# Turning activation rows on TensorE instead of by DMA, and folding late row pairs before the transform back over p

## The chip, the core and the metric

The kernel runs on one core of one Trainium2 chip. The metric is the device time of one execution in microseconds (us). Runs of one kernel agree here within some tenths of a per cent.

## The reference, cut to what matters

Two kinds of layer, A and B, alternate on a state `x` of 2048 rows and 512 columns in bfloat16: A, B, A, B. A is a two-dimensional Fourier filter, B is a small MLP that mixes neighbouring rows.

```python
def _A_ref(x, w_r, w_i):
    X = rfft2(x) * (w_r + 1j * w_i)
    return irfft2(X, s=(S, D))

def _B_ref(x, w1, w2, w3, w4):
    h = gelu(layernorm(x) @ w1)
    # g0..g3: the four column quarters of h, shifted by -1, +1, -2, +2 rows
    x1 = x + concatenate([g0, g1, g2, g3]) @ w2
    return x1 + gelu(layernorm(x1) @ w3) @ w4

x = x + _A_ref(layernorm(x)); x = x + _B_ref(layernorm(x))
x = x + _A_ref(layernorm(x)); x = x + _B_ref(layernorm(x))
```

## The kernel before, in words

The 2048 rows are written as 16 p + q with 128 values of p (the partitions) and 16 values of q. A "row" below is one q: a tile of 128 partitions by 512 columns. The state `K.x` holds the 16 rows in SBUF for the whole run.

`first_front` makes the first half of the first Fourier transform; then `layer` runs twice, each time finishing an A and doing a B, and the first run also makes the front of the next A. One run of `layer` goes through these stages:

- The filter: `over_d`, `over_q`, the product with `W` in `weigh`, `back_q`, and copies out of PSUM between them.
- The way back. `back_d` (L662) makes four rows of columns for a pair of rows in two PSUM banks: an even part in the first 256 columns and an odd part in the last 256. `take_D` copies the pair to SBUF as `Y`. `back_p` (L690) transforms a row back over p with four matmuls of 256 columns: the left half of the row is even plus odd part, the right half even minus odd, and both sums are formed in PSUM. `add_x` (L698) adds to the state, `stats2` (L303) squares on ScalarE, `rstd2` forms the inverse deviation on GpSimd, and `norm2` (L400 on VectorE and GpSimd, L402 on ScalarE) makes the normalized row `xn`.
- The turn. A matmul contracts over partitions, so the normalized rows must be turned so that the columns of the row lie on the partitions. `tr` (for `w1`) and `tr3` (for `w3`) call `turn` for a pair of rows, and `turn` issues one DMA transpose on SyncE's queue (L718) from `xn` into `xT`. There are 8 of each in a layer.
- The MLP. `w1` (L733), `gelu1` (L740), `w2` (L749), `add_x1` (L757), `square3`, `rstd3`, `norm3`, then `w3` (L784) with `gelu3` (L791) and `w4` (L804) with `add_x2` (L810) and, in the last layer, `store` (L814).
- In the first run of `layer`, scaled tables (`scale_T`, L410/L412) and `front` (L429, L439) of the next A are interleaved with the last matmuls of `w4`.

Nothing is scheduled by the compiler. Three strings, `ORDER_0`, `ORDER_A` and `ORDER_B`, list the operations by one letter and a number, and each engine executes its own operations in that order. A trailing A, V, P or D names the engine, and ".b" names the first PSUM bank. The letters used below: D and C `back_d`, Y `take_D`, P `back_p`, a `add_x`, s `stats2`, n `norm2`, T `tr`, v `w1`, h `gelu1`, u `w2`, U `tr3`, w `w3`, W `w4`. X is `fill`: so many matmuls on a zero tile (L274) whose result nobody reads. Every engine waits for its inputs in order, so one instruction that waits holds up all that stand behind it on its engine.

The options `half_D` (K) and `fold_D` (H) stand in the kernel before but are not used: `FOLD` is empty for both layers.

Of the kernel before, what the change touches and what calls it, by code (L numbers as in the profile page):

```python
# [28 lines left out]
def dft_tables():  # L29
# [12 lines left out]
    p = np.arange(P)  # L42
    pair = lambda j, s: (j if s == 0 else 64 - j) if j else 32 * s
    T = np.zeros((P, NH, 2, 2))
    for j in range(NH):
        for s in range(2):
            i = pair(j, s)
            T[:, j, s, 0] = np.cos(2 * np.pi * i * p / 128)
            T[:, j, s, 1] = np.sin(2 * np.pi * i * p / 128) if i else np.cos(np.pi * p)
    T = T.reshape(P, P)  # L50
    d = np.arange(D // 2)
    f = np.arange(1, 257)
# [9 lines left out]
    w = np.full(256, 2.0)  # L62
    w[255] = 1.0
    G = np.stack([cos * w, sin * w]) / (S * D)
    G = G.transpose(2, 0, 1).reshape(2, P, 2, D // 2).transpose(1, 0, 2, 3)
    A = np.zeros((NH, NQ, 2, 2, 2, 32))
    B = np.zeros((NH, NQ, 2, 2, 2, 32))
    q = np.arange(NQ)
    for j in range(NH):
        for sg in range(2):  # L70
            for m in range(32):
                k = 64 * m + (j if sg == 0 else 64 - j if j else 32)
# [24 lines left out]
           "Tinv": np.stack([T.T, -T.T], axis=1)}  # L97
# [43 lines left out]
def banks(K, n):  # L141

    k = K.bank
    if k is None:
        k = K.next_bank if K.next_bank + n <= 8 else 0
        K.next_bank = (k + n) % 8
    return K.ps[:, k:k + n, :]


def copy(K, dst, src, eng):  # L150
    if eng == "V":
        K.nc.vector.tensor_copy(dst, src)  # L152
    else:
        K.nc.scalar.activation(dst, src, ACT.Copy, bias=0.0, scale=1.0)  # L154


def load_all(K, A_x, A_w_r, A_w_i, B_w1, B_w2, B_w3, B_w4):
# [16 lines left out]
    for pl, v in enumerate(planes):  # L174
        nc.scalar.dma_start(K.W[2::4, pl, 0], v[:, 32])
    for lo in range(0, NH, 8):
        for pl, v in enumerate(planes):
            load_W(K, v, pl, lo, lo + 8)
    K.TL = K.const.tile([P, 2, NB, P], BF16, name="TL")
# [28 lines left out]
    def load_mlp():  # L208
        gate2 = K.const.tile([1, 16], BF16, name="gate2")
        nc.sync.dma_start(gate2[:], K.W[1:2, 1, NH - 1, 1:17])  # L210
        for k in ("G", "Tinv"):
            table(k, nc.sync)
        for k, w, n, c in (("w1", B_w1, 4, D), ("w2", B_w2, 4, D), ("w3", B_w3, 4, FH), ("w4", B_w4, 14, D)):
            t = K.const.tile([P, n, c], BF16, name=k)
            setattr(K, k, t)
            if k != "w4":
                load_halves(t, w, n)

    def load_w4():
        load_halves(K.w4, B_w4, 14)  # L220

    def load_halves(t, w, n):
        v = w.rearrange("(t p) n -> p t n", p=P)
        for part in (slice(0, n // 2), slice(n // 2, n)):
            nc.sync.dma_start(t[:, part], v[:, part])

    K.load_w4 = load_w4
# [10 lines left out]
def load_W(K, v, pl, lo, hi):  # L238


    j1 = max(lo, 1)
    fwd, rev = [K.W[2 * sg::4, pl] for sg in range(2)]
    K.nc.sync.dma_start(fwd[:, lo:hi], v[:, lo:hi])
    K.nc.sync.dma_start(rev[:, j1:hi], v[:, 65 - hi:65 - j1][:, ::-1])
# [243 lines left out]
def first_front(K):  # L488
# [66 lines left out]
    dummy = K.const.tile([P, 1, P], BF16, name="dummy")  # L555
    K.nc.sync.dma_start_transpose(dummy[:], K.zeros[:])
# [11 lines left out]
def layer(K, last):  # L568
# [144 lines left out]
    def turn(to, k, rows):  # L713

        g, h = divmod(k, 2)
        if g not in to:
            to[g] = K.grp.tile([P, 4, 4, P], BF16, name="xT", bufs=4)
        nc.sync.dma_start_transpose(to[g][:, 2 * h:2 * h + 2].rearrange("p q t c -> p (q t) c"),  # L718
                                    rows.rearrange("p q d -> p (q d)"))

    def tr(k):
        turn(xT, k, xn[:, 2 * k:2 * k + 2, :])
        turned.append(k)
        if len(turned) == 8 and not last:
            K.load_w4()
# [48 lines left out]
    def tr3(k):  # L774
        q = ROWS[2 * k]
        turn(xT3, k, xn[:, q:q + 2, :])
# [84 lines left out]
    def act_table(k):  # L861
# [4 lines left out]
    next_V, turned = {}, []  # L866
    table = {"z": act_table, "e": lambda g: ln[g].std_twice(), "i": lambda g: ln[g].invert_twice(), "M": lambda g: ln[g].shift(), "J": invert4, "d": over_d, "t": take_d, "q": over_q, "x": take_q, "p": weigh, "b": lambda b: back_q(b, first_half(b)), "V": lambda b: back_q(b, 1),
             "D": lambda m: back_d(m, 0), "C": lambda m: back_d(m, 1), "Y": take_D, "P": back_p, "a": add_x, "s": stats2, "r": rstd2, "c": lambda g: ln[g].ratio(), "n": norm2,
             "T": tr, "v": w1, "h": gelu1, "u": w2, "f": add_x1, "k": square3, "E": resid,
# [34 lines left out]
FLEX = "mlGLnotxYIKEpQ"  # L904
FOLD = [(), ()]
ORDER_0 = """
s1 f0 s0 s3 s2 i3 i2 i0 s4 s5 S1 J1 s7 S0 J0 s6 i7 f2 Q2A Q3A i4 Q0A s9 i6 s8 O1.2 s11 f3 S2 J2 Q6P Q1A Q5A O0.4 i8
G1A Q4V O2.0 s10 i11 i10 S3 Q7P O3.2 G0A s13 J3 Q10V Q11A s12 s14 i12 O5.6 i14 G3A i13 G2A Q8P Q9P s15 S4 J4 O4.4 G5A
i15 Q12V Q13V S5 O6.0 L5A J5 Q14P O7.6 G4A G6A G3V Q15V L6V G7A O8.0 L7A G8A I3V L8A
"""  # L910
ORDER_A = """
d0.3 t0A d2.4 d1.2 d4.0 q0.6 t1V N0 t2A q1.2 d6.4 t4A q2.0 x1V x0V p1V t6A q4.2 d12.6 d10.4 x2A p2P p0V t12A t10A d8.0
p4D b0.6 d14.7 q10.4 m0V q6.2 t8A x10A t14A b1.0 b5.1 m5A m1A q12.4 q14.6 p6D b4.1 b2.0 p10V x14A p14P d15.2 m4A m2A
t15A q8.6 x8A b3.1 b7.0 m7A b11.2 q15.6 m11A x15A b10.3 b14.0 m3A b6.2 m6A p12D V12.4 b12.5 p8V p15V b13.7 b9.1 m10A
m12A b8.6 b15.2 m13V V15.3 m14V m9A m8V V13.5 V14.0 m15A D1.6 l12V D0.1 l15A l13A l14V C1 C0 Y0V Y1A D3.3 C3 P3.0 a3
P2.6 Y3A a2 s3 P0.5 a0 s2 P1.2 a1 s0 D2.0 C2 Y2V s1 r0 D5.6 C5 P7.2 a7 Y5A e0 s7 P6.4 D7.0 P4.5 a6 i0 M0 P5.2 D4.6 C4
P10.3 s6 C7 n2P a4 s4 a5 n3V n0V s5 Y4A D6.4 r1 P11.2 C6 P8.6 P9.7 e1 n1V a10 T1 Y7A P15.0 i1 M1 n5A s10 n4P n6P P14.1
Y6V P13.3 a8 s8 T0 a9 n7P s9 a11 P12.4 a15 s11 v1.6 r2 n10P T2 h1 T3 a13 a12 n11V c0 s15 T5 n8V v0.2 h0 s13 v3.4 n9V
v2.2 h3 u0.0 s12 h2 u1.4 a14 c1 s14 T4 u3.1 r3 f0 k0 n14V v5.2 n13A n15V T7 f1 E1V h5 f3 v4.6 u2.0 f2 E2V h4 c2 u6.6
f6 u5.5 f5 E5V k3 E6V n12P u7.0 E0V u4.1 f4 T6 v7.5 k2 k1 R0 E3V o2V o1V h7 o3A c3 v6.1 h6 o0P f7 u8.0 f8 E8P u13.5  # L920
u12.2 u11.6 u14.3 U1 f12 k4 k5 k7 f14 E14V k12 k6 u9.2 f11 u10.4 k8 E7V f13 k13 f10 R1 o7P o5P u15.3 E10V U0 w4.0 E4P
f9 E9P k11 f15 w2.4 g2 k10 o4V U2 w1.2 k14 g4 E15P k9 E13P w3.6 g3 g1 w5.0 w0.4 g0 w6.6 g5 g6 E11V W1.2 o6P U3 E12V A1
W3.6 A3 B3 B1 w8.0 W2.4 A2 W0.2 k15 R2 o10P o11A R3 o14V o9A g8 o12A w13.0 U5 w7.6 B2 g13 o8P U4 w15.4 w10.0 A0 B0 g10
w16.2 j1 g7 g16 w18.0 g18 w9.2 o15P w11.0 g9 w12.2 g12 j3 w17.6 j2 j0 S0 Q3V Q1V Q2P Q0V g11 W4.2 U7 O1.0 o13P g17 U6
A4 W7.3 B4 j4 G1A G1V A7 B7 j7 O0.0 w19.6 G0A W6.2 A6 g19 W5.3 A5 g15 B5 w23.4 g23 j5 B6 j6 S1 Q4P G0V w27.2 g27 I0V
w14.6 g14 Q5V O2.0 w20.2 w24.6 g20 W10.2 A10 B10 Q7V j10 W8.3 G2A A8 B8 W9.4 A9 B9 Q6V j9 W11.2 A11 w26.4 I1P B11 j11
g24 j8 O3.2 w22.6 S2 Q10P g26 G2V I2P Q11A Q8P g22 w21.0 g21 G3A w25.6 G3V g25 W12.0 A12 B12 j12 Q9P S12 J12 I3P O4.5
G4A Q12A G4V W15.1 A15 I4P B15 j15 W13.2 A13 S15 J15 B13 j13 W14.3 Q15P W24.2 S13 J13 Q13P O5.0 A14 A24 B14 B24 j14
G5A O15.4 G15V O6.2 S14 J14 L15A Q14A O14.4 G6A L6A G14A G5V I5V L14A
"""  # L930
# [47 lines left out]
```

## Time and profile before

| | us |
|---|---|
| median of three runs | 343.75 (343.66 to 343.83) |
| the profiled execution | 343.63 |
| its span, first to last instruction | 341.8 |
| TensorE (PE) busy | 334.3 (98%) |
| ScalarE (ACT) busy | 192.0 |
| VectorE (DVE) busy | 163.5 |
| GpSimd (POOL) busy | 117.5 |

The profiled execution takes 1.83 us more than its span. The busy time of PE is a sum over pipelined matmuls whose ends are modelled, so what a matmul costs is better read from the distance between the starts of consecutive ones. The granted TensorE clock is 1.000 in the whole execution.

The parts of the span, by the starts of PE's stages:

| stretch, us | work of PE |
|---|---|
| 0 to 18.96 | first front |
| 18.96 to 36.85 | filter of the first layer |
| 36.85 to 51.16 | way back up to the first `w1` |
| 51.16 to 79.08 | `w1`, `w2` |
| 79.08 to 181.59 | `w3`, `w4`, front of the next layer |
| 181.59 to 199.36 | filter of the second layer |
| 199.36 to 214.57 | way back up to the first `w1` |
| 214.57 to 242.37 | `w1`, `w2` |
| 242.37 to 341.8 | `w3`, `w4`, stores |

### The profile page before, as it was taken

The numbers are of one execution on the slowest core, as the hardware profiler recorded it, in microseconds if no ns is written. First come the engines' busy times: TensorE is split into PE (matmuls) and PEld (weight loads), VectorE is DVE, ScalarE is ACT, GpSimd is POOL, SyncE is SP. The second block draws the span as 40 slices with busy tenths as digits, with TensorE's granted clock in tenths as the row PEclk, the third lists the DMA queues.
The fourth block names the chain that finished last, engine by engine and source line by source line (L and its number), as shares of the span: only waits on it lengthen the run. The fifth ranks groups of instructions, "written<-read, shape, count | busy, mean of one in ns | idle before, by whom it ended". The sixth has DMA issues, their size and how long they took to land.

```text
span 341.8 us, 5734 instructions
## 1 busy us (share of the span) xinstructions
PE 334.3 (98%) x2184; PEld 186.8 (55%) x2184; DVE 163.5 (48%) x373; ACT 192.0 (56%) x356; POOL 117.5 (34%) x218
## 2 busy tenths in 40 slices
PE   6999999999999999999999999999999999999996
PEld 4878984444444444444467898444444444444443
DVE  4979895659034023535378979456901110200112
ACT  6989899665821542421628979986695132142310
POOL 3795067669633000402432505877722000000000
PEclk9999999999999999999999999999999999999999
DMA  7985936390231100000000003543130500000011
GB/s 261 313 284 197 339 78 117 71 270 19 46 61 31 32 0 0 2 0 0 2 0 2 2 3 64 104 83 61 33 61 0 125 31 0 15 17 32 15 63 46
DMA packets 45340, 24.60 MB, mean 72 GB/s; under 512 B 35153, under 2 KB 42321, under 8 KB 45313
## 3 DMA queue, kind: packets, MB, share of 16 engines
q1 hardware_dynamic: 43824, 19.74, 23.0%
q0 software_dynamic: 1248, 4.40, 3.9%
q8 instruction: 17, 0.28, 0.3%
q10 hardware_dynamic: 240, 0.10, 0.1%
q14 instruction: 11, 0.08, 0.1%
HBM read 11.61 MB, written 2.10 MB: 40 GB/s over the span
## 4 chain that ended last, share of the span: by engine, by line
PE 85%; ACT 8%; DVE 3%; DMA 2%; issue 1%; SPq 0%; ACTq 0%
PE ps L804 28%; PE ps L784 28%; PE ps L749 8%; PE ps L733 6%; PE ps L642 4%; ACT xn L303 3%; PE ps L612 2%; PE ps L594 2%; DVE x_state L698 2%; PE ps L662 2%; DMA x_state<-in_A_x_dram 1%; ACT hT L740 1%; DMA xT<-xn 1%; PE ps L439 1%; PE ps L429 1%
## 5 line engine op out<-in xcount | busy, mean ns | idle before, releaser
L791 ACT ACTIVATE gT<-ps 128x1024 bf16<-128x1024 f32 x56 | 55.7, 1023 | 97.6 <-PE ps L784 95.5
L804 PE MATMUL ps<-w,gT 128*128 128x512 bf16 (+2 forms) x476 | 99.4, 366 | 0.0
L784 PE MATMUL ps<-xT,w 128*128 128x512 bf16 x448 | 99.3, 379 | 0.0
L810 DVE TENSOR_TENSOR x_state<-ps,x_state 128x512 bf16<-128x512 f32 (+2 forms) x34 | 22.1, 659 | 123.4 <-PE ps L804 123.1
L804 PEld LDWEIGHTS <-gT 128*128 128x128 bf16 x476 | 45.4, 98 | 51.4
L784 PEld LDWEIGHTS <-w 128*128 128x128 bf16 x448 | 43.7, 98 | 52.1
L757 DVE SCALAR_TENSOR_TENSOR xn<-xn,ln_c,ps 128x512 bf16<-128x512 bf16 x32 | 23.3, 742 | 16.0 <-PE ps L749 6.3
L733 PE MATMUL ps<-xT,w 128*128 128x512 bf16 x128 | 28.6, 379 | 0.4 <-DMA xT<-xn 0.4
L749 PE MATMUL ps<-w,hT 128*128 128x512 bf16 x128 | 28.8, 379 | 0.1
L326 POOL TENSOR_SCALAR ln_ve<-ln_mv 128x4 f32<-128x4 f32 x11 | 3.0, 271 | 57.7 <-DVE ln_mv L319 57.0
L303 ACT ACTIVATE junk<-xn 128x512 bf16<-128x512 bf16 x32 | 19.8, 623 | 5.0 <-DVE xn L757 5.0
L291 DVE BATCH_NORM_STATS2 ln_st<-x_state 128x6 f32<-128x512 bf16 (+2 forms) x30 | 19.5, 665 | 3.5 <-DMA x_state<-in_A_x_dram 3.0
L698 DVE SCALAR_TENSOR_TENSOR x_state<-ps,x_state 128x512 bf16<-128x512 f32 x32 | 20.6, 684 | 0.9 <-PE ps L690 0.9
L733 PEld LDWEIGHTS <-w 128*128 128x128 bf16 x128 | 12.4, 98 | 15.6 <-DMA xT<-xn 1.0
L749 PEld LDWEIGHTS <-hT 128*128 128x128 bf16 x128 | 12.5, 98 | 15.4 <-ACT hT L740 1.0
L303 ACT ACTIVATE xn<-x_state 128x512 bf16<-128x512 bf16 x32 | 19.9, 626 | 0.8 <-DVE x_state L698 0.8
L740 ACT ACTIVATE hT<-ps 128x512 bf16<-128x512 f32 x32 | 17.6, 600 | 4.6 <-PE ps L733 4.5
L690 PE MATMUL ps<-Y,Tinv 128*128 128x256 bf16 x128 | 15.8, 272 | 0.4 <-DVE Y L152 0.4
L631 POOL TENSOR_TENSOR PB<-X,W 128x2048 bf16<-128x2048 bf16 (+1 forms) x4 | 12.1, 3033 | 11.2 <-DVE X L152 7.3
L154 ACT ACTIVATE TV<-ps 128x1024 bf16<-128x1024 f32 (+1 forms) x17 | 14.6, 895 | 2.4 <-PE ps L594 2.3
L642 PE MATMUL ps<-TR,PB 128*128 128x128 bf16 x256 | 15.9, 219 | 0.0
L662 PE MATMUL ps<-G,hT 128*128 128x256 bf16 x128 | 15.6, 273 | 0.0
(96 smaller groups left out, 414.0 us busy)
## 6 DMA issues: line engine op xcount, KB each, us to landing
w<-in_B_w_dram SPq DMA_DIRECT2D x4, 896.0 KB, 7.0
W<-W POOLq DMA_DIRECT2D x4, 514.0 KB, 5.1
x_state<-in_A_x_dram SPq DMA_DIRECT2D x8, 256.0 KB, 4.9
out_dram<-x_state SPq DMA_DIRECT2D x15, 128.0 KB, 1.8
w<-in_B_w_dram SPq DMA_DIRECT2D x4, 256.0 KB, 4.4
W<-in_A_w_r_dram SPq DMA_DIRECT2D x7, 128.5 KB, 5.4
W<-in_A_w_i_dram SPq DMA_DIRECT2D x7, 128.5 KB, 5.6
TL<-tab_TL POOLq DMA_DIRECT2D x3, 256.0 KB, 5.5
```

The source lines that it names most:

```text
L303: K.nc.scalar.activation(out, src, ACT.Square, bias=0.0, scale=D ** -0.5, accum_out=self.s[:, i, 1:2])
L642: nc.tensor.matmul(o[:, k0 * P:(k0 + 1) * P], lhsT=pab[u][:, k, 2 * (b - u) + h, f * P:(f + 1) * P], rhs=K.TR[:, k:k + 2, 2 * b + h], star ...
L662: nc.tensor.matmul(o[:, i, e * 256:(e + 1) * 256], lhsT=M[:, F, e, 2 * m + i, :], rhs=K.G[:, F, e, :], start=(F == 0 and e == 0), stop=(F ...
L698: nc.vector.scalar_tensor_tensor(K.x[:, q, :], ps.pop(("P", q)), 1.0, K.x[:, q, :], op0=ALU.mult, op1=ALU.add, accum_out=ln[g].s[:, i, 0:1])
L733: nc.tensor.matmul(o[:, i], lhsT=K.w1[:, t, j * P:(j + 1) * P], rhs=xT[g][:, :, t, :], start=(t == 0), stop=(t == 3))
L740: nc.scalar.activation(hv[:, 2 * h + i, 4 * g:4 * g + 4, PAD:PAD + P], o[:, i].rearrange("p (q c) -> p q c", q=4), ACT.Gelu_apprx_tanh, bi ...
L749: nc.tensor.matmul(o, lhsT=K.hT[:, j, st:st + P], rhs=K.w2[:, j, :], start=(j == 0), stop=(j == 3))
L757: nc.vector.scalar_tensor_tensor(xn[:, q, :], xn[:, q, :], ln[q // 4].c[:, q % 4:q % 4 + 1], ps.pop(("u", n)), op0=ALU.mult, op1=ALU.add, ...
L784: nc.tensor.matmul(o[:, i], lhsT=K.w3[:, c, t * P:(t + 1) * P], rhs=xT3[g][:, :, c, :], start=(c == 0), stop=(c == 3))
L791: nc.scalar.activation(gT[g][:, 2 * j:2 * j + 2, :], ps.pop(("w", k)), ACT.Gelu_apprx_tanh, bias=0.0, scale=1.0)
L804: nc.tensor.matmul(o, lhsT=gT[g][:, t, i * P:(i + 1) * P], rhs=K.w4[:, t, d], start=(t == 0), stop=(t == 13))
L810: nc.vector.tensor_tensor(x, ps.pop(("W", n)), x, op=ALU.add)
```

## The change

`turn` no longer issues a DMA. It runs eight matmuls for a pair of rows: each has a block of 128 by 128 of `xn` as the stationary operand and a new 128 by 128 identity table `unit` as the moving one, and the turned pair lies in two PSUM banks. A new operation (Z for `tr`, F for `tr3`) copies the two banks to `xT` on ScalarE or VectorE.

`FOLD` becomes (4, 5, 6, 7) in both layers. For these row pairs, `half_D` copies the odd part to SBUF in float32 and `fold_D` forms sum and difference on VectorE, in place of `take_D`; `back_p` then needs two matmuls of 256 columns instead of four.

On the queues: the two small loads of `W` (16 KB each) move from ScalarE's queue to SyncE's, behind the first four loads of `W`; the load of `w4` moves from behind the eighth transpose to directly behind the load of `w3`; the dummy transpose goes; the load of `unit` (32 KB) is added before the weights. SyncE's queue then holds only loads and the final stores.

All three order strings are written anew. Apart from Z, F, K and H the operations are the same; some move to another engine and many to another place.

```diff
-           "Tinv": np.stack([T.T, -T.T], axis=1)}
+           "Tinv": np.stack([T.T, -T.T], axis=1), "unit": np.eye(P)}
...
-    for pl, v in enumerate(planes):
-        nc.scalar.dma_start(K.W[2::4, pl, 0], v[:, 32])
     for lo in range(0, NH, 8):
         for pl, v in enumerate(planes):
             load_W(K, v, pl, lo, lo + 8)
+        if lo == 0:
+            for pl, v in enumerate(planes):
+                nc.sync.dma_start(K.W[2::4, pl, 0], v[:, 32])
...
-        for k in ("G", "Tinv"):
+        for k in ("G", "Tinv", "unit"):
             table(k, nc.sync)
...
-            if k != "w4":
-                load_halves(t, w, n)
-
-    def load_w4():
-        load_halves(K.w4, B_w4, 14)
+            load_halves(t, w, n)
...
-    dummy = K.const.tile([P, 1, P], BF16, name="dummy")
-    K.nc.sync.dma_start_transpose(dummy[:], K.zeros[:])
...
-    def turn(to, k, rows):
-
-        g, h = divmod(k, 2)
+    def turn(key, rows):
+
+        ps[key] = o = banks(K, 2)
+        for i in range(2):
+            for t in range(4):
+                nc.tensor.matmul(o[:, i, t * P:(t + 1) * P], lhsT=rows[:, i, t * P:(t + 1) * P], rhs=K.unit[:],
+                                 start=True, stop=True)
+
+    def take_turned(to, key, eng):
+        g, h = divmod(key[1], 2)
         if g not in to:
             to[g] = K.grp.tile([P, 4, 4, P], BF16, name="xT", bufs=4)
-        nc.sync.dma_start_transpose(to[g][:, 2 * h:2 * h + 2].rearrange("p q t c -> p (q t) c"),
-                                    rows.rearrange("p q d -> p (q d)"))
+        copy(K, to[g][:, 2 * h:2 * h + 2].rearrange("p q t c -> p q (t c)"), ps.pop(key), eng)
 
     def tr(k):
-        turn(xT, k, xn[:, 2 * k:2 * k + 2, :])
-        turned.append(k)
-        if len(turned) == 8 and not last:
-            K.load_w4()
+        turn(("T", k), xn[:, 2 * k:2 * k + 2, :])
...
-        turn(xT3, k, xn[:, q:q + 2, :])
+        turn(("U", k), xn[:, q:q + 2, :])
...
-FOLD = [(), ()]
+FOLD = [(4, 5, 6, 7), (4, 5, 6, 7)]
```

The new order of the first layer, from the first `back_d` to the first `w2`:

```
D1.4 l12V C1 D0.0 C0 D3.2 Y1A P3.6 a3 Y0A C3 D2.4 C2 s3 Y2A Y3V P1.6 P0.7 a1 P2.3 a0 s1 P6.2 a2 P4.6 a6 s0 s2 D5.4 C5
a4 K5A P7.3 a7 r0 D4.0 e0 i0 M0 n2P s6 s7 H5 P5.2 n3P C4 K4A X7.7 P10.3 T1.4 D7.6 a5 C7 H4 P9.2 s4 s5 Z1A n1V n0P T0.0
r1 K7A a10 e1 D6.4 C6 Z0A a9 P11.3 i1 M1 n5P K6A H7 n4P P8.2 H6 n6P v1.0 T2.6 n7P c0 P15.4 h1 a11 s9 a8 s8 P12.5 P13.3
a13 T3.0 Z3V v0.2 a15 Z2A s11 s10 P14.0 r2 a12 s12 a14 v3.6 h3 v2.0 h0 u0.4
```

and of the second, from the first `back_d` to the first `w1`:

```
D0.4 l15V l13A D2.0 l14A C0 C2 Y2A D1.2 C1 Y0V D3.6 C3 P4.1 P5.0 Y1V P3.2 Y3A P7.3 a4 s4 P6.4 a5 s5 D5.0 a7 s7 P2.5
a6 s6 P0.3 a3 a0 C5 r1 D4.6 s3 a2 P1.2 K5A a1 e1 i1 M1 s2 D7.4 s1 C7 C4 K4A n6P H5 X5.3 P10.2 s0 r0 n7V T3.0 H4 a10
n4A e0 i0 X6.3 P8.3 a8 n5P T2.6 P11.2 Z3A a11 M0 n0P Z2A K7A D6.0 C6 P9.3 n1V T0.6 n3P n2P a9 H7 v2.2
```

The fills are X6 at the head of the second layer before, and X3 (head of the first layer), X7, X5 and X6 after.

## The prediction

> **What bounds the kernel now.** I read the page first: the shares of the engines, the slices, then the chain that ended last.
>
> ```profile
> span 341.8 us, 5734 instructions
> PE 334.3 (98%) x2184; PEld 186.8 (55%) x2184; DVE 163.5 (48%) x373; ACT 192.0 (56%) x356; POOL 117.5 (34%) x218
> PE   6999999999999999999999999999999999999996
> PEclk9999999999999999999999999999999999999999
> PE 85%; ACT 8%; DVE 3%; DMA 2%; issue 1%; SPq 0%; ACTq 0%
> ```
>
> PE is busy in every slice but the first and the last, at full clock, and carries 85% of the chain. Busy alone could be matmuls that wait inside their pipeline, so I then took the distances between matmul starts, from the chain of waits in order of time:
>
> ```profile
> 142.44 0.45 PE ps L439 x8
> ...
> 160.60 5.18 PE ps L784 x24
> ...
> 181.59 0.66 PE ps L274 x6
> ...
> 202.15 0.90 PE ps L690 x8
> ```
>
> So 128 moving columns cost 56 ns (0.45/8), 256 cost 110 ns (0.90/8, 0.66/6), 512 cost 216 ns (5.18/24): cost goes with the columns, and a weight load of its own for each matmul (L439 has one too) does not show. PE is at its streaming rate. What is left of waiting inside the run is seen in PE's timeline:
>
> ```profile
> 48.21 2.80 PE L690 MATMUL ps<-Y,Tinv 128*128 128x256 bf16 x24
> 51.16 7.08 PE L733 MATMUL ps<-xT,w 128*128 128x512 bf16 x32 [0.15 <-DMA xT<-xn]
> ...
> 204.61 2.35 PE L662 MATMUL ps<-G,hT 128*128 128x256 bf16 x20
> 207.40 1.64 PE L690 MATMUL ps<-Y,Tinv 128*128 128x256 bf16 x12 [0.44 <-DVE Y L152]
> ...
> 211.50 2.78 PE L690 MATMUL ps<-Y,Tinv 128*128 128x256 bf16 x24
> 214.57 7.08 PE L733 MATMUL ps<-xT,w 128*128 128x512 bf16 x32 [0.29 <-DMA xT<-xn]
> ```
>
> From start to start, less the matmuls between at 109 to 110 ns, PE lost 0.3 us at 51.16, 0.6 at 207.40 and 0.4 at 214.57. Only the first and third are waits for a transpose. The waits table agrees on how little the transposes cost, and shows that ScalarE and VectorE wait for PE and not the other way round:
>
> ```profile
> DVE x_state L810 <- PE ps L804: 123.1, 27, 16.8
> ACT gT L791 <- PE ps L784: 95.5, 35, 12.8
> PEld L733 <- DMA xT<-xn: 1.0, 2, 0.6
> PE ps L733 <- DMA xT<-xn: 0.4, 2, 0.3
> ```
>
> The page's PE idle is 341.8 - 334.3 = 7.5 us; 1.0 of it lies before the first matmul, 1.9 + 0.5 + 0.3 in the front, 2.7 after the last matmul. About 1.1 us is left for the whole middle (a few tenths more when counted by starts). So nearly every matmul that is added must be paid, and nearly none can be hidden.
>
> **The change part by part.**
>
> *The turns on TensorE.* 8 T and 8 U in each of two layers are 32 turns of 8 matmuls, 256 in all, 128 moving columns each. By the L439 row (same operand sizes, own weights each time): 32 x 0.45 = 14.4 us. The 16 U stand among L784 and L804, where PE is busy without a gap from 79 to 181 and from 242 to 339 us: 7.2 us on the path in full. The 16 T stand among `back_p`, `w1` and `w2`, where PE is also busy in full but for the waits above: another 7.2. The nearest rule is in the Trainium skill, "TensorE: Matmul & The Clock Gate", Part 4 (PE-mode transpose): in its transpose mode about 275 ns for 128x128 in a kernel, and not counted as activity by the clock gate. By that, 256 x 0.275 = 70 us, with a cold clock on top. But the diff issues plain matmuls against an identity, and the row for such a shape says 56 ns at a clock of 1.00; the 219 ns that the same row gives as the mean of one L439 matmul is its latency, which overlaps. I take 14.4; its lower end is the same, since 128 columns cannot stream faster than the row, and its upper end 14.9 (L642, also 128 columns: 3.68 us for 64 at 33.19, 57.5 ns).
>
> *What the turns take away.* 32 DMA transposes, 3.1 us each to landing, and the dummy. They are off PE's path but for the 0.3 and 0.4 us above. The skill's "VectorE: DVE Perf Modes" (The three transpose paths) gives 1309 ns by DMA against 390 ns on TensorE for a 128x128 block and advises TensorE. By that, 256 x 0.92 = 235 us would be gained if all of it were waited for; the trace shows 0.4 us of PE waiting in 2 of 32. What is late next: turn, latency and copy are about 0.45 + 0.2 + 1.0 = 1.7 us against 3.1 to 3.5, so a `w1` can start about 1.5 us earlier only where its inputs were last; PE's own work then fills that place. The 0.7 us are set against the new waits below.
>
> *Copies out of PSUM.* 32 copies of 128x1024 float32 to bfloat16: 17 on ScalarE (like Y at L154, 1.01 us) and 15 on VectorE (L152, 1.22): 17 and 18 us. The 16 F lie where both engines mostly wait for PE (L791 and L810 above): nothing, covered by w3 and w4; if that cover were gone, 1 to 1.2 us each. The 16 Z lie in the stage from 36.85 to 79.08, where ScalarE is busy 33.7 of 42.2 us and VectorE 29.6; with 4.6 to 5 us more each they stay below PE, but around the first `w1` ScalarE has no slack (12.8 of 14.3 us).
>
> *The fold.* 16 rows lose two matmuls of 256 columns: 32 x 0.11 = 3.5 us less on PE, on the path. In place of 4 casts Y (1.0 to 1.2) per layer come 4 K (128x512 float32, like `right`, 0.59) and 8 halves of H (like L461, 0.68): some 3.5 us more per layer, on VectorE mostly. Cover: PE's deferred `back_p` (P8 to P15 now stand around and behind the first T and v).
>
> *Fills.* X7, X5 and X6 stand inside the way back: 18 x 0.11 = 2.0 us. PE executes them, so they are paid whether a wait would stand there or not. X3 at the head and the X6 that goes from the head of layer two lie in waits for the last copy of V (0.3 us idle at 18.96): nothing, either way; without them the wait remains.
>
> *New waits.* Walking the new order of layer one with the durations above from the first D: last `a` of rows 0 to 3 at 6.4 us, its square at 7.05, deviation and normalized rows 2 and 3 (both on GpSimd, 0.77 each) at 10.0; PE has 9.7 us of work before T1 (12 D/C x 0.44, 8 P x 0.44, 7 fills, one folded P): 0.3 us of wait. ScalarE then has K7, e1 and Z0 before v1 and ends at 14.1, PE is there at 13.6: 0.5. Through the table load (1.28) and h1, s, Z2, h3 to h0, which u0 needs: ScalarE 23.2, PE 22.85: 0.4. So 1.2 us against 0.6 before (0.3 at 51.16 and 0.3 among the L749 ahead of 60.95). In layer two T3 must wait for n7V, which stands behind H5: 11.4 against 10.35 of PE, 1.0 us; before it was 0.6 + 0.2 + 0.4. Both layers together: + 0.6 - 0.2 = + 0.4. These waits aren't in the trace: lower end -1.4 (all old ones go, none comes), upper end +4 (each of the four places in each layer later by half a square or copy, 0.5).
>
> *Queues and front.* ScalarE issues two DMAs less (L175, 1.2 us of its queue) but its first work waits for x, landing at 3.9 us: nothing; an earlier landing gives up to 0.2. SyncE's queue gets them, 1.2 us more of issue before the last W (issued to 17.8, doubled copies landed by 31.2): W for `weigh` and G, needed at 36.85 and landed at 34.7, keep 1 us of margin; if that goes, up to 1 us. `unit` (32 KB) and w4 go ahead of nothing that is needed sooner. The front has the same work in another order: 0, ±0.5.
>
> **Sum**, against the profiled 343.63 (span 341.8 + 1.83): + 14.4 (turns) - 3.5 (fold) + 2.0 (fills) + 0.4 (waits, new less old) = 356.9. The profiled execution lies 0.12 below the median of the runs shown: nothing to correct.
>
> **The rivals.**
> 1. *The work is as counted, the waits go* (0.22). The fills sit where waits would be and everything old is given back: 343.63 + 14.4 - 3.5 + 2.0 - 1.4 = 355.1; with half of the fills replaced by a better flow, 353.5 at the least. For it: fewer PE operations ahead of the first v. Against: ScalarE and VectorE get more work there.
> 2. *ScalarE and VectorE become the bound of the way back* (0.19). K, H and Z come when ScalarE was busy 12.8 of 14.3 us. If half of the additional 4.8 us per layer is not covered, + 2 x 2.4: about 361; with PSUM banks held longer, 364.
> 3. *Not slower* (0.02). TensorE would have to take the turns into time that it lost to the transposes: 14.4 + 2.0 - 3.5 = 12.9 us, 0.40 us for each turn. It decides from 12.9 us of hidden waiting; the trace has 0.3 + 0.4 by the starts and 7.5 in all. Were matmul ends hiding so much, L784 would not step at 216 ns. Time: 343.6 or less. That the turns are cheaper in some unseen way is in this chance.
>
> The likeliest (0.57) is 355.8 to 358.8. Range: 353.5 to 361.0, which holds rival 1 and the lower part of rival 2. A difference of 0.2% (0.7 us) is about what a measurement of this kernel tells from none. Faster 0.01, same 0.01, slower 0.98.
>
> **What would show it.** PE busy still 97 to 98%; a new group of 256 matmuls with `unit`, 8 in 0.45 us; L690 with 96 instead of 128; no DMA_TRANSPOSE; the stretches with w3 and w4 longer by 3.6 us per layer each; the way back plus w1/w2 longer by 3.6 - 1.75 + fills + waits, some 3.5 per layer; PE waits of 0.3 to 1 us ahead of T1, v1, u0 and T3, released by GpSimd or ScalarE. Wrong would be: turns at more than 60 ns each, idle of PE over 3 us in a way back, U waiting for a norm or a bank in the w3 stage, or a front that ends more than 1 us from 18.96.

## The result and the profile after

The changed kernel takes 358.31 us (median of four runs, 357.93 to 358.83); the kernel before took 343.71 us on the same chip (343.62 to 343.83). The ratio is 1.0425, with a 95% interval of 1.0407 to 1.0443. The change makes the kernel slower by 14.6 us. The prediction said 356.9 us and slower, in a range of 353.5 to 361.0.

The profiled execution of the changed kernel took 358.05 us, with a span of 356.3; before these were 343.63 and 341.8. The page of the changed kernel:

```profile
span 356.3 us, 6168 instructions
PE 348.0 (98%) x2423; PEld 199.6 (56%) x2423; DVE 186.0 (52%) x390; ACT 207.4 (58%) x376; POOL 115.3 (32%) x227
PE   6999999999999999999999999999999999999996
PEclk9999999999999999999999999999999999999999
PE 84%; ACT 8%; DVE 5%; issue 2%; DMA 1%; POOL 0%; DVEq 0%; ACTq 0%; POOLq 0%
```

The picture is that of before: PE is busy in every slice but the first and the last, at full clock, and carries 84% of the chain. Only the span is 14.5 us longer, and the number of matmuls has grown by 239: 256 for the turns, less 32 for the fold, and 21 fills in place of 6. Now the chain of waits of the changed kernel, in order of time, where two turns for `w3` stand between the `w3` themselves:

```profile
99.81 0.45 PE ps L711 x8
...
106.30 1.73 PE ps L780 x8
108.03 0.45 PE ps L711 x8
108.47 1.73 PE ps L780 x8
```

L711 is a turn, L780 `w3`. The second number is what the step took: eight matmuls of a turn take 0.45 us, whatever stands around them, and the `w3` step at the same 216 ns as before. Nothing overlaps: the chain goes from one to the other. The groups of the changed kernel by shape (busy time, mean ns of one):

```profile
L711 PE MATMUL ps<-unit,xn 128*128 128x128 bf16 x256 | 19.7, 219 | 0.3 <-POOL xn L395 0.2
L683 PE MATMUL ps<-Y,Tinv 128*128 128x256 bf16 x64 | 8.1, 273 | 0.0
L678 PE MATMUL ps<-Y,Tinv 128*128 128x256 bf16 x32 | 5.7, 272 | 0.0
```

The whole way back over p has 96 matmuls instead of 128 (the folded rows are L678, two each). The mean of 219 ns of a turn's matmul is its latency; its price is the 56 ns from one start to the next.

The parts of the span, by the starts of PE's stages. "Streaming" is the number of matmuls times their step (56 ns for 128 columns, 109 for 256, 163 for 384, 216 for 512; the half-height matmuls of `over_q` run two at a time, so a pair counts 109); "rest" is the length less that, so waits and all else. "Fills" are the X, which are in neither.

| stage | before, us | rest | after, us | rest |
|---|---|---|---|---|
| first front | 18.96 | | 19.21 | |
| filter, layer one | 17.89 | 1.97 | 17.84 | 1.92 |
| way back to the first `w1` | 14.31 | 0.34 | 13.83 | 0.82, and 0.76 of fills |
| `w1`, `w2` | 27.92 | 0.29 | 32.77 | 0.70 |
| `w3`, `w4`, next front | 103.00 | 0.30, and 0.66 of fills | 105.35 | 0.62 |
| filter, layer two | 17.28 | 1.36 | 18.14 | 2.22 |
| way back to the first `w1` | 15.21 | 1.24 | 14.91 | 1.02, and 1.20 of fills |
| `w1`, `w2` | 27.64 | 0.01 | 30.86 | 0.10 |
| `w3`, `w4` | 96.89 | 0.16 | 100.43 | 0.16 |
| after the last matmul | 2.70 | | 2.96 | |

The stages behind the filters, where streaming and rest are both counted, grew by 12.1 us of streaming and fills (256 turns' matmuls 14.3, fold -3.5, fills 1.96 - 0.66) and by 1.1 of rest; the two filters, the front and the end grew by 1.3 together. That is the 14.5. A stage does not hold the same work before and after: in each layer only six of the eight turns for `w3` stand in the `w3`, `w4` stage, the other two stand ahead of the first `w3`; and in layer two four matmuls of `w2` (0.86 us) have come to stand behind the first `w3`.

Where PE still waits is seen in its timeline of the changed kernel, around the way back of layer one and of layer two. The columns are start and length in us, then the group; a bracket is the idle time before it and what ended it:

```profile
45.87 0.93 PE L269 MATMUL ps<-zeros 128*128 128x256 bf16 x7
46.63 0.48 PE L678 MATMUL ps<-Y,Tinv 128*128 128x256 bf16 x2
46.95 0.92 PE L711 MATMUL ps<-unit,xn 128*128 128x128 bf16 x8
...
50.16 0.60 PE L678 MATMUL ps<-Y,Tinv 128*128 128x256 bf16 x4
50.88 1.89 PE L729 MATMUL ps<-xT,w 128*128 128x512 bf16 x8
...
72.38 1.90 PE L729 MATMUL ps<-xT,w 128*128 128x512 bf16 x8 [0.27 <-DVE xT L152]
...
216.87 0.71 PE L269 MATMUL ps<-zeros 128*128 128x256 bf16 x5
...
217.77 0.61 PE L711 MATMUL ps<-unit,xn 128*128 128x128 bf16 x8
...
219.28 0.38 PE L711 MATMUL ps<-unit,xn 128*128 128x128 bf16 x4
219.82 0.40 PE L711 MATMUL ps<-unit,xn 128*128 128x128 bf16 x4 [0.16 <-POOL xn L395]
...
222.04 1.89 PE L729 MATMUL ps<-xT,w 128*128 128x512 bf16 x8
```

By the starts, 0.30 us are lost inside the turn at 46.95, 0.28 ahead of the `w1` at 50.88 (50.16 and four steps of 109 ns make 50.60), 0.43 before 72.38, 0.32 between the two halves of the turn at 219.28 and 0.19 inside the one at 221.39. The turn at 217.77, the first of layer two, does not wait. The waits table of the changed kernel (us in total, times, longest) agrees that these are small, and shows what hides the new copies:

```profile
DVE x_state L806 <- PE ps L800: 107.7, 24, 14.4
ACT gT L787 <- PE ps L780: 81.4, 33, 7.3
PEld L729 <- DVE xT L152: 0.8, 1, 0.8
PEld L711 <- POOL xn L395: 0.6, 2, 0.3
```

VectorE waited 123.1 us for `w4` before and waits 107.7 now, ScalarE 95.5 us for `w3` before and 81.4 now: the copies F have gone into time in which both waited for PE anyway.

### The profile page after: what moved, and what is told of

The parts are those of the page before. It is cut to its first block, busy times and chain, and to the rows that moved or that the text cites. A ratio compares the mean times of both kernels' runs of the same rounds, so it can differ in the third digit from the quotient of the medians.

```text
span 356.3 us, 6168 instructions
## 1 busy us (share of the span) xinstructions
PE 348.0 (98%) x2423; PEld 199.6 (56%) x2423; DVE 186.0 (52%) x390; ACT 207.4 (58%) x376; POOL 115.3 (32%) x227
## 2 busy tenths in 40 slices
DMA packets 11534, 16.25 MB, mean 46 GB/s; under 512 B 1344, under 2 KB 8512, under 8 KB 11504
## 4 chain that ended last, share of the span: by engine, by line
PE 84%; ACT 8%; DVE 5%; issue 2%; DMA 1%; POOL 0%; DVEq 0%; ACTq 0%; POOLq 0%
PE ps L800 27%; PE ps L780 27%; PE ps L729 8%; PE ps L745 7%; PE ps L635 4%; PE ps L711 4%; ACT xn L298 3%; PE ps L605 2%; PE ps L655 1%; PE ps L587 1%; DMA x_state<-in_A_x_dram 1%; DVE Y L152 1%; ACT V L154 1%; DVE PB L621 1%; PE ps L434 1%
## 5 line engine op out<-in xcount | busy, mean ns | idle before, releaser
L787 ACT ACTIVATE gT<-ps 128x1024 bf16<-128x1024 f32 x56 | 55.8, 1021 | 81.5 <-PE ps L780 81.4
L800 PE MATMUL ps<-w,gT 128*128 128x512 bf16 (+2 forms) x476 | 100.5, 366 | 0.0
L780 PE MATMUL ps<-xT,w 128*128 128x512 bf16 x448 | 99.8, 379 | 0.0
L806 DVE TENSOR_TENSOR x_state<-ps,x_state 128x512 bf16<-128x512 f32 (+2 forms) x34 | 22.0, 657 | 107.8 <-PE ps L800 107.7
L780 PEld LDWEIGHTS <-w 128*128 128x128 bf16 x448 | 43.7, 98 | 51.9
L745 PE MATMUL ps<-w,hT 128*128 128x512 bf16 x128 | 30.4, 379 | 0.0
L729 PE MATMUL ps<-xT,w 128*128 128x512 bf16 x128 | 29.4, 379 | 0.4 <-DVE xT L152 0.3
L152 DVE CAST xT<-ps 128x1024 bf16<-128x1024 f32 x15 | 18.3, 1218 | 14.5 <-PE ps L711 14.5
L154 ACT ACTIVATE xT<-ps 128x1024 bf16<-128x1024 f32 x17 | 17.3, 1020 | 8.5 <-PE ps L711 8.5
L286 DVE BATCH_NORM_STATS2 ln_st<-x_state 128x6 f32<-128x512 bf16 (+2 forms) x30 | 19.6, 665 | 3.8 <-DMA x_state<-in_A_x_dram 3.4
L711 PEld LDWEIGHTS <-xn 128*128 128x128 bf16 x256 | 16.7, 98 | 7.1 <-POOL xn L395 0.6
L729 PEld LDWEIGHTS <-w 128*128 128x128 bf16 x128 | 12.3, 98 | 14.4 <-DVE xT L152 0.8
L711 PE MATMUL ps<-unit,xn 128*128 128x128 bf16 x256 | 19.7, 219 | 0.3 <-POOL xn L395 0.2
L304 POOL TENSOR_SCALAR ln_mv<-ln_s 128x4 f32<-128x4 f32 x16 | 4.3, 268 | 47.4 <-DVE x_state L691 37.9
L621 DVE TENSOR_TENSOR PB<-ps,W 128x1024 bf16<-128x1024 f32 x15 | 17.8, 1218 | 0.0
```

Source lines behind the costliest of these rows:

```text
L621: nc.vector.tensor_tensor(t[:, :, 2 * i:2 * i + 2], o[:, :, i * 256:(i + 1) * 256].unsqueeze(1).to_broadcast([P, 2, 2, 256]), K.W[:, :, 2 ...
L711: nc.tensor.matmul(o[:, i, t * P:(t + 1) * P], lhsT=rows[:, i, t * P:(t + 1) * P], rhs=K.unit[:], start=True, stop=True)
L729: nc.tensor.matmul(o[:, i], lhsT=K.w1[:, t, j * P:(j + 1) * P], rhs=xT[g][:, :, t, :], start=(t == 0), stop=(t == 3))
L745: nc.tensor.matmul(o, lhsT=K.hT[:, j, st:st + P], rhs=K.w2[:, j, :], start=(j == 0), stop=(j == 3))
L780: nc.tensor.matmul(o[:, i], lhsT=K.w3[:, c, t * P:(t + 1) * P], rhs=xT3[g][:, :, c, :], start=(c == 0), stop=(c == 3))
L787: nc.scalar.activation(gT[g][:, 2 * j:2 * j + 2, :], ps.pop(("w", k)), ACT.Gelu_apprx_tanh, bias=0.0, scale=1.0)
```

## The experiments

Seven kernels with one part of the change doubled or undone come first, then the parts put into the orders of before, and last a mixture.

**The turns for `w3` twice.** Each of them runs its eight matmuls two times into the same banks.

```diff
-        for i in range(2):
+        for n in range(2 * 2 if key[0] == "U" else 2):
+            i = n % 2
```

> The changed kernel with each of the 16 turns ahead of w3 (U) run twice: 128 matmuls of 128 columns more, none of whose results is new. Theory A: 128 x 56 ns = + 7.2, 365.5. Theory B says the same here (PE has no gap in the w3 stage). If turns could hide in pipeline latency or gaps of PE: less than + 4.

Measured: 365.10 us (364.99 to 365.65), ratio 1.061 (1.059 to 1.0629). That is 6.8 us more than the changed kernel, where 128 matmuls at 56 ns are 7.2. By the stages it is 2.68 us in each `w3`, `w4` stage, where six of the eight turns stand, and 0.89 and 0.90 in `w1`, `w2`, where the other two stand: 7.15 in all. These turns are paid in full.

**The turns for `w1` twice.** The same line with "T".

> The changed kernel with each of the 16 turns ahead of w1 (T) run twice. Theory A: + 7.2, less what falls into the waits of the two ways back (0.8 and 1.0 us there): + 5.5 to + 7.2, 363.8 to 365.5. Theory B (PE waits for copies there): the second pass goes into waits, and what comes later is the latency of T alone: + 2 to + 4, 360.3 to 362.3.

Measured: 363.75 us (363.37 to 363.96), ratio 1.0565 (1.0542 to 1.0588), 5.4 us more. Here 1.7 us are missing from 7.2. By the stages about 1.0 of it went into the waits of the ways back: the rest falls from 0.82 to 0.49 and from 1.02 to 0.34. Another 0.6 went into the waits among `w1` and `w2` of layer one. So a small part of a turn for `w1` can be hidden, as long as there is a wait behind it.

**The turns for `w3` by DMA**, as in the kernel before, all else as after.

```diff
-        turn(("U", k), xn[:, q:q + 2, :])
+        turn_dma(xT3, ("U", k), xn[:, q:q + 2, :])
```

> The changed kernel with the 16 turns ahead of w3 (U) made by DMA transposes; the 16 T stay on TensorE. Theory A (turns paid in full, latency hidden in the w3 stage): - 7.15, 351.2. Theory C (the new order leaves less room than a transpose takes; the run with all turns by DMA lost 3 to 4 us of waits in the two w3 stages): 354 to 355.5.

Measured: 353.12 us (352.94 to 353.73), ratio 1.0265 (1.0249 to 1.0280), 5.2 us less than after, between the two expectations. The two stretches with `w3` and `w4` become shorter by 2.2 and 2.26 us, where their six turns each are worth 2.7. The largest piece of the missing 2 us is a wait for a transpose that lands too late for the new order: the first `w3` of layer two waits for it (1.6 us from its weight load on), and with that the rest of the `w1`, `w2` stage ahead of it grows from 0.10 to 1.38.

**No fold**: `FOLD` empty, K becomes Y on the same engine, H goes.

```diff
-FOLD = [(4, 5, 6, 7), (4, 5, 6, 7)]
+FOLD = [(), ()]
...
-... C5 a4 K5A P7.3 a7 r0 D4.0 e0 i0 M0 n2P s6 s7 H5 P5.2 ...
+... C5 a4 Y5A P7.3 a7 r0 D4.0 e0 i0 M0 n2P s6 s7 P5.2 ...
```

> The changed kernel without the fold: K becomes one cast Y of the pair on the same engine, H goes, FOLD is empty, back_p of rows 8 to 15 has four matmuls again. Theory A: + 32 x 0.11 = + 3.5, less up to 1 us of waits behind H (n7V, Z0): 360.8 to 361.8. Theory B: ScalarE and VectorE lose 3.5 us of work per layer and give it back: 357 to 359.

Measured: 361.59 us (361.14 to 362.17), ratio 1.0505 (1.0484 to 1.0527), 3.3 us more than after. The fold saves 32 matmuls of 256 columns, 3.5 us at 109 ns. In the new orders it gives back what its matmuls cost. The waits of the two ways back are not of its making: without it the rest there is 1.00 and 1.13 us, no less than with it (0.82 and 1.02).

**No fills** X7, X5 and X6 in the ways back.

> The changed kernel without the fills X3, X7, X5 and X6 (21 matmuls on a zero tile that nobody reads). Theory A, as booked in the prediction (PE pays for them): - 2.0, 356.3. Theory B (they stand where T1, T3 and T2 wait for a normalized row anyway; the trace after shows 0.3, 0.3 and 0.2 us of wait right behind them): 0 to - 0.3, 358.0 to 358.3.

Measured: 358.00 us (357.64 to 359.30), ratio 1.0411 (1.0384 to 1.0439): no difference to the changed kernel. PE's timeline of this kernel at the place where the seven fills stood:

```profile
46.30 0.27 PE L678 MATMUL ps<-Y,Tinv 128*128 128x256 bf16 x1 [0.22 <-DVE Y L670]
...
46.90 0.27 PE L678 MATMUL ps<-Y,Tinv 128*128 128x256 bf16 x1 [0.33 <-DVE Y L670]
47.01 0.91 PE L711 MATMUL ps<-unit,xn 128*128 128x128 bf16 x8
```

Counted from the first `back_d`, the turn starts 0.2 us later than with the fills (10.10 against 9.90). Where the fills were, PE now waits for H on VectorE. The rest of the two ways back becomes 1.79 and 2.21 us and their lengths 14.04 and 14.90 (13.83 and 14.91 with fills). So the fills cost nothing here: they stand in waits that are there without them.

**The filter of layer two in its old order**, all else as after. In the new order GpSimd makes none of the products of `weigh`.

```diff
-d1.1 t1V d15.7 t15A d4.2 d0.5 t0V q1.0 p1D t4A q15.6 d12.4 q0.2 x15A ... V15.6 D0.4 l15V l13A D2.0 l14A C0 ...
+X6.7 d4.4 d15.7 t15A d12.2 t4V d1.0 d0.1 q15.4 t1V q4.6 t12A x15V ... m11A l12A D0.4 l15V l13A D2.0 C0 ...
```

> The changed kernel with the filter stage of the second layer (from its first over_d to its first back_d) in the order of the kernel before, with its X6 at the head. Theory D (the new order of this stage itself lost 0.9 us: 18.14 against 17.28 us from the first over_d to the first back_d): - 0.7 to - 1.0, 357.4. Theory E (the stage is longer because of what comes before it, the last copies of V): 358.3 as it is.

Measured: 357.88 us (357.04 to 360.23), ratio 1.0411 (1.0370 to 1.0451). The runs scatter by more than the difference that was looked for, so the time alone does not decide. The stage does. From the windows of the filter of layer two: first the kernel with the old order, then the changed one (length, busy time of PE, weight load, VectorE, ScalarE, GpSimd, clock, DMA share, GB/s):

```profile
188.99:206.12 17.13, 17.13 (x259) 14.60 (x256) 16.03 (x17) 15.83 (x26) 6.35 (x2) 1.00 0.01 2
```

```profile
189.00:207.13 18.13, 17.79 (x256) 14.86 (x257) 16.50 (x18) 17.01 (x29) 0.00 (x0) 1.00 0.01 2
```

The new order takes 1.0 us longer. GpSimd does nothing in it, where it made two products of 3.2 us each, and ScalarE is busy 17.01 of 18.13 us. PE waits for ScalarE there, at the longest place 0.40 us by the starts; the rest of the 1.0 us is spread:

```profile
198.16 1.53 PE L605 MATMUL ps<-TV,TL 64*128 64x256 bf16 x24 [0.24 <-ACT TV L154]
```

This loss comes from the order of the stage and not from turns or fold, which both kernels have. Not all of it is won back: the six fills X6 of the old order make the stage before longer by 0.35.

**All turns by DMA**, new orders, fold and fills kept; Z and F do nothing.

> The changed kernel with all 32 turns made by DMA transposes again (T and U issue one on SyncE's queue, Z and F do nothing, the dummy transpose is back); new orders, fold and fills stay. Theory A (PE's streaming time is the bound, turns are paid in full): 358.3 - 14.3 = 344.0, plus up to 4 us where the new orders leave less time than the 3.1 us of a transpose: 344 to 348. Theory B (the copies Z on ScalarE and VectorE hold the way back): with the copies gone too, below 343.5.

Measured: 354.82 us (353.70 to 356.53), ratio 1.0312 (1.0276 to 1.0348). Both expectations missed: 14.3 us of PE's work are gone, and only 3.5 us came back. PE waits in their place: of the 10.8 us that did not come back, the ways back and the `w1`, `w2` stages hold 9.5, some 2.4 in each of the four. A row of its waits in this kernel, then its timeline, then one row of the chain:

```profile
PE ps L740 <- DMA xT<-xn: 4.4, 4, 1.9
```

```profile
52.60 2.78 PE L740 MATMUL ps<-xT,w 128*128 128x512 bf16 x8 [1.86 <-DMA xT<-xn]
55.17 1.49 PE L680 MATMUL ps<-Y,Tinv 128*128 128x256 bf16 x6
```

```profile
49.40 3.06 DMA xT<-xn
```

A transpose lands 3.1 us after its release. The new order leaves a turn the time of its matmuls (0.45 us) and of one copy (1.02 on ScalarE, 1.22 on VectorE), so the first `w1` (L740) waits 1.9. And those eight `w1` take 2.57 us to the next start instead of 1.73. The windows tell why (columns as above; the clock is the third from the end):

```profile
50.03:53.44 3.41, 1.37 (x8) 0.51 (x6) 3.41 (x10) 1.88 (x2) 2.96 (x5) 1.00 0.44 82
53.44:56.85 3.41, 3.41 (x12) 1.66 (x11) 0.69 (x3) 2.03 (x5) 2.20 (x6) 0.50 0.82 153
56.85:60.27 3.42, 3.42 (x18) 1.65 (x17) 2.47 (x8) 2.92 (x9) 1.42 (x4) 1.00 0.00 0
```

Behind the wait the granted clock is a half for 3.41 us, in which PE is busy throughout; the steps of `w1` go from 215 to 427 ns. Lost are 3.41 x 0.50 = 1.7 us, almost as much as the wait itself.

**Fold alone**, in the orders of before with DMA transposes: Y of rows 4 to 7 becomes K on ScalarE with H directly behind.

```diff
-... P7.2 a7 Y5A e0 s7 ... a5 n3V n0V s5 Y4A D6.4 ...
+... P7.2 a7 K5A H5 e0 s7 ... a5 n3V n0V s5 K4A H4 D6.4 ...
```

> The kernel before, with its own orders and DMA turns, and the fold alone: FOLD for the pairs 4 to 7 of both layers, each of their Y replaced by K on ScalarE and H. Theory A (PE bound, work paid in full): - 3.5, 340.2. Theory B (3.5 us per layer more on ScalarE and VectorE, which are busy 12.4 to 12.8 of 14.3 us there): the copies come later than back_p wants them, waits of 1 to 2 us per layer: 342 to 345.5.

Measured: 354.83 us (354.33 to 355.24), ratio 1.0310 (1.0295 to 1.0326). 3.5 us less of matmuls, and 10.9 us slower than before; both expectations missed. PE's timeline of this kernel, then VectorE's:

```profile
49.97 0.61 PE L685 MATMUL ps<-Y,Tinv 128*128 128x256 bf16 x4 [1.66 <-DVE Y L677]
52.10 0.70 PE L685 MATMUL ps<-Y,Tinv 128*128 128x256 bf16 x4 [1.52 <-DVE Y L677]
55.13 0.37 PE L685 MATMUL ps<-Y,Tinv 128*128 128x256 bf16 x1 [2.33 <-DVE Y L677]
```

```profile
54.39 1.29 DVE L677 TENSOR_TENSOR Y<-ps,half 128x512 bf16<-128x512 f32 x2 [2.26 <-ACT half L154]
```

A folded row needs two engines one after the other, K 0.6 us and H 1.3, where Y needed one. VectorE takes its instructions in order, waits 2.3 us for K in front of H, and everything behind H waits with it. The ways back grow to 19.6 and 19.4 us. The clock falls here too; its mean over the run is 0.985.

**Turns alone**, and **the turns for `w3` alone**, in the orders of before without fold. Each copy is put directly behind its turn, in a bank that is free by the order there:

```diff
-... n1V a10 T1 Y7A P15.0 ...
+... n1V a10 T1.0 Z1A Y7A P15.0 ...
```

> The orders of the kernel before and no fold, but all 32 turns on TensorE: each T and U gets two PSUM banks that are free at its place (T1 and T2 of the first layer stand one to a few operations later for that), and its copy Z or F follows it at once, on the engine that the changed kernel uses. Theory A (turns paid in full): + 14.3, plus waits of T for rows that were normalized just before it (a DMA queue waited there before, now PE does): 343.8 + 14.3 + 1 to 5 = 359 to 363, more than the whole change, so new orders and fold together earn 1 to 5 us. Theory F (orders and fold are worth nothing): 358 as the whole change.

> As the run with the turns alone, but T is made by DMA transposes as in the kernel before: only the 16 turns ahead of w3 are on TensorE, in the orders before, without the fold. Theory A: + 7.2, plus 0 to 2 for waits of U for its row and for w3 waiting for the copy: 351 to 353. If turns could hide anywhere: below 349.

Measured: 418.94 us (418.36 to 421.08), ratio 1.2202 (1.2167 to 1.2237), and 382.02 us (380.81 to 382.78), ratio 1.1123 (1.1105 to 1.1142). Expected were 15 to 19 and 7 to 9 us more; it was 75 and 38. Part of it is seen in PE's timeline of the second kernel:

```profile
114.01 0.61 PE L713 MATMUL ps<-unit,xn 128*128 128x128 bf16 x8
115.94 1.89 PE L791 MATMUL ps<-xT,w 128*128 128x512 bf16 x8 [1.31 <-DVE xT L152]
117.66 0.61 PE L713 MATMUL ps<-unit,xn 128*128 128x128 bf16 x8
119.59 4.69 PE L791 MATMUL ps<-xT,w 128*128 128x512 bf16 x21 [1.32 <-DVE xT L152]
```

Behind each of these turns PE waits 1.3 us for the copy on VectorE, because the next `w3` writes the bank that holds the turned rows (in the order, `U5.6 F5V w7.6` and `U4.4 F4V w15.4`). To see whether the banks were all of it, a third kernel moved the turns for `w3` to banks whose next writer comes latest, some of them one operation later:

```diff
-... k10 o4V U2.6 F2V w1.2 ...
+... k10 o4V w1.2 U2.4 F2V ...
```

> As the run with U alone on TensorE in the orders before (382.0), with two things moved and nothing else: each U takes the pair of free PSUM banks whose next writer comes latest (in that run it mostly took the pair that the next w3 or front wanted), and where the room allows stands one large PE operation later. T stays on DMA, no fold. Theory H (the 31 us beyond the 7.2 us of the turns were banks: the next writer on PE waited 1.3 to 3.6 us for the copy F): 352 to 356. Theory G (the orders before cannot take turns on PE, whatever the banks): 370 or more.

Measured: 383.24 us (380.14 to 385.89), ratio 1.1109 (1.1041 to 1.1176). No gain, so the choice of the bank alone is not the cause. (In the profiled execution PE is at half clock for six stretches of 3.4 us, against three in the run before; by the work that stands in them this costs some 4 us more, an estimate, and does not bring the time near the 352 to 356 us that were expected if it were the banks.) The longest of its waits, in PE's timeline, and the windows around it:

```profile
268.04 14.50 PE L791 MATMUL ps<-xT,w 128*128 128x512 bf16 x56 [5.64 <-ACT xT L154]
```

```profile
262.00:268.00 6.00, 0.40 (x8) 0.32 (x5) 5.90 (x16) 4.17 (x10) 3.68 (x10) 0.82 0.00 0
268.00:275.00 7.00, 6.96 (x22) 2.65 (x22) 1.48 (x4) 1.07 (x2) 2.46 (x5) 0.67 0.00 0
```

The first `w3` of the second layer waits 5.6 us for a copy that stands in ScalarE's queue, and the clock then costs 7.00 x 0.33 = 2.3 us more. That the rest of the 38 and 75 us is of this kind, copies queued in order behind late work, is likely, but it was not taken apart further, and the places were chosen for these experiments. What these kernels do show: in neither of the two placements do the orders of before take the turns for `w3` without some 30 us beyond their own 7.2.

**A version put together from the parts**: the turns for `w3` and for the last four pairs of `w1` by DMA, no fills, the old order in the filter of layer two.

> The changed kernel with what the runs so far recommend put together: U and the last four T of each layer by DMA, only the first four T (ahead of the first w1) on TensorE, no fills, the filter stage of the second layer in its old order. From the run with U by DMA (353.1): - 1.0 (filter) - 8 x 0.45 (T) + 1 to 3 (waits of w1 for transposes as in the run with all turns by DMA) = 349.5 to 351.5. A version that beats the kernel before (343.8) would need the waits to be none and 6 us more.

Measured: 355.74 us (353.82 to 356.19), ratio 1.0341 (1.0310 to 1.0371). It was expected to be the best one of the changed ones and is slower than the kernel with only the turns for `w3` by DMA. Its waits on PE begin with

```profile
PE ps L740 <- DMA xT<-xn: 2.8, 2, 2.6
```

a `w1` that waits 2.6 us for a transpose which lands later than the copy for which the order was made. A stretch at half clock follows (67.44 to 70.85). Three of its four executions have a mean clock of 0.994 or 0.995; the fourth, at 0.999, took 353.82 us, still no better than 353.12. No version was faster than the kernel before.

## Why the prediction was right, point by point

- **PE is the bound, and what is added is paid.** Right. The kernels with turns doubled cost 6.8 and 5.4 us of 7.2 each. Taken by stages, the doubled turns for `w3` cost 7.15 of 7.17.
- **Turns + 14.4, fold - 3.5.** Both right in size: 256 x 56 ns = 14.3 us, and 3.3 measured by taking the fold away.
- **The stretches with `w3` longer by 3.6 in each layer.** Right as a sum over the layer, wrong in the place. The 16 U do not all stand among `w3` and `w4`: two of eight stand ahead of the first `w3` in each layer, so only 2.7 us fall there. Layer one grew by 2.35, because six fills (0.66) left its end and waits grew by 0.3. Layer two grew by 3.54, close to 3.6 by coincidence: 2.7 of turns and 0.86 of `w2` that moved there. For the way back with `w1` and `w2` the prediction said "some 3.5", where its own terms (3.6 - 1.75 + 1.0 of fills + 0.2 of waits) make 3.05; measured are 4.4 and 2.9. All four together grew by 13.2, where the sum had 13.3.
- **Fills + 2.0, "paid whether a wait would stand there or not", and new waits + 0.4.** This is the step that was wrong as a cause, though not in the sum. Without fills the time stays the same: PE then waits for H in their place, and the waits of the two ways back are 1.79 + 2.21 = 4.0 us, against 0.34 + 1.24 = 1.6 before. So the new order waits 2.4 us longer there, and the fills only lie in these waits. The 2.0 and the 0.4 were booked as work and wait; their sum comes out near the 2.4 because the walk through the new order had been made with the fills in place.
- **Copies out of PSUM at nothing.** Nearly right: F lies in the waits of ScalarE and VectorE for PE; of Z, two are waited for, 0.28 us ahead of 50.88 (booked as the wait of v1) and 0.43 before 72.38.
- **Rival 2 (ScalarE and VectorE as bound of the way back)** fell in its size, 358.3 against about 361, but not in kind. That the two ways back are shorter than before (13.83 and 14.91 us against 14.31 and 15.21) says little, as they hold less work of PE. Their waits, fills counted as such, grew by 0.48 + 0.76 in layer one and by 1.20 - 0.22 in layer two, 2.2 us; that is no more than the 2.4 that were booked as fills and new waits, with nothing of the 4.8 that the rival puts on top. But without the fills VectorE is what PE waits for there.
- **New waits at T1 0.3, v1 0.5, u0 0.4, T3 1.0.** Measured 0.30, 0.28, none to speak of, and none. The longest wait of layer two, 0.32, is inside T2 (219.28), for a row normalized on GpSimd, and was not foreseen; nor was the one of 0.43 at 72.38: a copy Z on VectorE stood behind a sum of `resid` that took three times as long as usual (below).
- **"Front 0, ±0.5", and the filters at nothing because the operations are the same.** The front grew by 0.25 and the end behind the last matmul by 0.26; that is within the bounds. The filter of layer two grew by 0.86, which the prediction did not price at all: of the new order's places outside the ways back it looked at the front only. With its old order the stage takes 17.13 instead of 18.14. These 0.86 are the largest piece of the 1.2 us by which the profiled execution (358.05) lies above 356.9.
- **Rival 1 (355.1, all waits go)** fell: waits grew. **Rival 3 (not slower)** fell by the doubled turns.
- **The skill's rules.** The 275 ns for a transpose on TensorE would have given 70 us; the matmul against an identity steps at 56 ns, at a clock of 1.00. The advice to transpose on TensorE ("VectorE: DVE Perf Modes", Rules for kernel authors) is borne out here for latency: 0.45 us and a copy of 1.02 or 1.22, against 3.06 by DMA. It was worth next to nothing because the 3.06 us were hidden, and it moved the work onto the one engine that had no room.

## What to carry to other kernels

Where one engine is busy in 98% of the span, ask of a shorter latency only how long that engine waits for it now, and charge every instruction put on it in full. An order written for one latency is part of the change: a piece taken out of it, or put into the old order, meets queues and waits that are made for something else, and can lose far more than the piece is worth. When an experiment opens a wait of some 2 us on TensorE, look at the granted clock behind it before explaining the time.

## What the runs showed of the hardware

- **The clock changes on a grid of 3.41 us.** In all 14 traces every change of the granted clock lies a whole multiple of 3.413 us after the trace's first one, and each stretch at half clock lasts 3.4 us or two or three times that. What counts is how much PE does in one stretch of that grid. In the kernel with all turns by DMA the stretch from 50.03 to 53.44 has PE busy for 1.37 of 3.41 us, and the next one is at half clock (windows above). The Trainium skill, "TensorE: Matmul & The Clock Gate" (What's actually happening), says the clock is halved after at least one idle window of about 3.4 us; here a stretch that was idle for 60% sufficed. Over the 14 traces, a full-clock stretch with PE busy for at most 40% was followed by half clock every time (12 of 12), one with 44 to 56% sometimes (3 of 13), a busier one never. What decides between 44 and 56% stays open. So a wait that falls across two stretches can pass unpunished, as in the front of the changed kernel, where PE idles 2.06 us:

```profile
8.01 2.14 PE L424 MATMUL ps<-Tq,x_state 128*128 128x256 bf16 x24 [2.06 <-ACT Tq L407]
10.62 1.59 PE L424 MATMUL ps<-Tq,x_state 128*128 128x256 bf16 x17 [0.47 <-ACT Tq L407]
```

```profile
4.12:7.53 3.41, 1.83 (x17) 1.48 (x16) 3.03 (x9) 3.12 (x11) 1.09 (x6) 1.00 0.97 321
7.53:10.94 3.41, 2.46 (x28) 2.13 (x28) 3.41 (x11) 3.41 (x11) 3.18 (x7) 1.00 1.08 366
```

  Behind this wait, up to 9.88, the matmuls of 256 columns start 109 ns apart and those of 128 columns (the row counts both) 56 ns; at half clock it would be 213 and more. Whether waits cost clock can differ between executions of one kernel: the four of the kernel with all turns by DMA have mean clocks of 0.994, 0.995, 0.999 and 1.000. Behind the front neither the kernel before nor the changed one waits for as long as 0.7 us in its profiled execution, and neither shows a drop there. At the head of the run the rows say 1.00, but the first fills of the kernel before step at 213 ns up to 4.83 us and at 109 ns from 4.96 on.
- **VectorE's sum beside GpSimd's.** Both ran a bfloat16 sum of 128x512 in `resid` at once:

```profile
67.03 0.46 DVE L760 TENSOR_TENSOR x_state<-x_state,xn 128x512 bf16<-128x512 bf16 x1
...
69.79 1.41 DVE L760 TENSOR_TENSOR x_state<-x_state,xn 128x512 bf16<-128x512 bf16 x1
```

```profile
69.76 1.15 POOL L760 TENSOR_TENSOR x_state<-x_state,xn 128x512 bf16<-128x512 bf16 x1
```

  The median of this sum on VectorE is 0.42 us; beside GpSimd's it took 1.41, and ended 0.3 us after GpSimd's end. In the kernel before, the two sums on VectorE that began while GpSimd's ran took 1.37 us each; in the changed one, the two that began 0.1 to 0.2 us ahead of it took 0.42. That fits the one that comes second being held until the other is done. It held up the copy Z behind it, and with that a `w1`.
- **The traffic.** With the transposes gone the DMA packets of a run fell from 45340 to 11534 and the bytes from 24.60 to 16.25 MB. No stage was seen to be shorter for it.
